# Three value loads put behind a later gate, and one copy put behind two loads, in a fused window-attention and feed-forward kernel

## The chip, the cores and the metric

The kernel runs on one core of a Trainium2 chip. The metric is the device time in microseconds (us) of one execution. Before the change three runs took 278.83, 281.04 and 281.4 us; the median is 281.04 us. The numbers of an engine's work come from one profiled execution.

The core has a matrix engine (TensorE, PE in the profile; its weight loads are PEld), a vector engine (VectorE, DVE), a scalar engine (ScalarE, ACT), a general engine (GpSimd, POOL) and a sync engine (SyncE, SP) that issues transfers. POOL and SP each work through their instructions in program order, and each issues DMAs (transfers) to a queue of its own. Both queues are served by the same 16 DMA engines.

## The reference

`q`, `k`, `v` have 8 batches, 8 heads, 576 positions and 64 values per head. Attention is limited to a window of 32 positions either side; its result, as 4608 rows of 512, goes through a two-layer feed-forward block:

```python
scores = q @ k.T / 8          # per batch and head
scores = where(abs(i - j) <= 32, scores, -1e9)
attn   = softmax(scores)
x      = (attn @ v).transpose(0, 2, 1, 3).reshape(4608, 512)
h      = x @ w_in                                  # 512 -> 2048
g      = h * sigmoid(1.702 * h)
out    = g @ w_out                                 # 2048 -> 512, float32
```

## The kernel before, in words

The 4608 rows are cut into 36 *units* of 128 rows and 9 *tiles* of 512 rows, four units each, numbered from 0. The kernel is one long program in which tile `t`'s first layer, tile `t-1`'s second layer and the attention of tile `t+1` are woven together by hand, so that PE always has something to multiply. The order on every engine is the order in which the program text emits it; waits are semaphores.

**Loads (POOL's queue).** For each unit, `load_kq` (line 144) brings 128 rows of queries or keys into a staging tile `qst` or `kst`, cast to 16 bits, and `load_v` (line 214) brings values into one of nine tiles `ve`. A unit that crosses a batch border takes two transfers. Each block of 64 queries needs keys and values of 128 positions, and the second block of a unit is offset by 64 rows; so values are needed a second time in shifted form: `odd_v(u)` (line 233) lets POOL copy half of unit `u`'s values and half of unit `u+1`'s into a tile `vo`, in two copies. It can run only when both units' values have landed.

**Transposes (SP's queue).** `turn(u)` has SP issue two DMA transposes (line 250): staged queries of `u` to `qT`, staged keys of `u+1` to `kT`. The normalized attention output `xn` is also transposed by SP's DMAs (line 447) into `xT`, four per tile, one per unit. SP's stores of finished output (line 613) stand in the same queue.

**A tile's round.** For `t` from 2 on, `front(t)` (not for `t = 2`) computes the scores of tile `t+1`'s four units, amid second-layer products, and emits `x_sums(t)` (lines 495 and 496): four DVE subtractions of quarters of `xT`, called `xs`, which the first layer of tile `t` multiplies. Then `back(t)` goes through four first-layer groups `n = 0..3` (`l1_group`). A group starts with a product from `xT`, then some second-layer work, then a product from `xs`. In group `n = 2` it first emits `values_four` (attention times values of tile `t+1`; `pv` in the profile, with `ve` and `vo` as operands), and `norm_four`, which normalizes into `xn` and emits the four `xT` transposes.

**The gates.** After a group, POOL makes a one-element copy `seen` (line 943) from a tile that DVE writes during the group (`gs`, line 510). POOL can't pass it before that group is that far. Behind the gate stand the loads of the table `LOADS`, by `(t, n)` or, where there is no such key, by `n`; the numbers in it count from `u = 4t + 4`. For `t = 2` (`u = 12`), ahead of the groups `n = 0` and `n = 1`, `ahead("kq", ...)` emits loads of queries 17 and keys 18, and of queries 18 and 19 with keys 19 and 20; just before `back(2)`, the three odd copies of units 13, 14 and 15.

The third tile is `t = 2`; its fourth group is `n = 3`. Units 12 to 15 are the attention of tile 3, units 16 to 19 that of tile 4. The first use of odd copy 15 is in `values_four(12)`; of values 16 to 20 and odd copies 16 to 19, in `values_four(16)`.

Of the kernel before, what the change touches and what calls it, by code (L numbers as in the profile page):

```python
# [26 lines left out]
class _Kernel:  # L27
# [689 lines left out]
    def opening(self):  # L717
# [95 lines left out]
        for u in (8, 9, 10, 11):  # L813
# [29 lines left out]
        self.x_T2(6, "t", act)  # L843
        self.do(self.l2, 5)

    LOADS = {(2, 1): [("kq", 8)], (2, 2): [("v", 5, 6, 7)], (2, 3): [("v", 8), ("kq", 9), ("odd", 4), ("kq", 10)],
# [25 lines left out]
    @staticmethod  # L872
    def do(fs, n=99):
        for _ in range(min(n, len(fs))):
            fs.pop(0)()
# [28 lines left out]
    def back(self, t):  # L904

        more = t + 1 < self.NT
        do, l2 = self.do, self.l2
        u = 4 * t + 4
        bands = [lambda i=i: self.band(u + i) for i in range(4)] if more else []
        dv = bands  # L910
        for n in range(4):
            for i in {2: ((4,), (5,), (6, 7), ()), 3: ((4, 5), (6, 7), (), (8,))}.get(t, ((5, 6), (7,), (), (8,)))[n]:
                self.turn(u + i)
            if t == 2:
                self.ahead("kq", *((17,), (18, 19), (), ())[n])
            if more and n == 2:
                self.values_four(u)
                self.norm_four(u, ("A", "C", "E"), (0, 1))
                do(l2, 1)

            key = n if more else ("last", n)
            if t == 2:
                key = ("first", n) if n < 2 else n
            share = dict(zip((1, 7, 2, 4), self.SHARES.get(key, (3, 3, 5, 5))))

            def fill(i):
                do(l2, share[i])
                self.l2eng = self.nc.scalar
                if i == 4 or more and (n, i) == (1, 7):
                    do(dv, 99 if i == 4 else 2)  # L930

            def side(i):
                if more and n == 2:
                    self.norm_four(u, (f"t{i}",), (2 + i,))
                else:
                    do(dv, 1)

            self.l1_group(t, n, fill, side)
            dv += self.g_sums(t, 2 * n, 2)
            if more and (t > 2 or n > 0):  # L940
                if u + n + 7 <= self.NU:
                    c = 2 * ((n - 1) % 4) + 1
                    self.nc.gpsimd.tensor_copy(self.seen, self.gs[t - (n == 0)][0:1, 2, c, 255:256])  # L943
                for what, *us in self.LOADS.get((t, n)) or self.LOADS[n]:
                    for i in us:
                        if what == "odd":
                            self.spread(u + i)
                        else:
                            self.ahead(what, u + i)
        return dv  # L950

    def run(self):
        pool, act = self.nc.gpsimd, self.nc.scalar
        self.l2eng, self.seed2 = self.nc.vector, act
        more = self.l2 = self.layer2_plain(0, 0) + self.layer2([(i, j) for i in range(self.NT) for j in range(2)][1:-1],
                                                               (self.NT - 1, 1))
        self.opening()
        self.do(self.x_sums(1))
        late = self.first_layer1()
        do = self.do  # L960
        dve = self.nc.vector
        do(more, 8)
        self.scores_two(8, ("t", "AC"))
        exps = self.scores(10, "BE", True)
        self.turn(14)
        self.turn(15)
        do(late)
        do(more, 4)
        self.band_two(8)
        self.l2eng = act  # L970
        do(more, 16)
        do(exps)
        do(more, 8)
        self.values(8, "t")
        self.values(9, "AC")
        self.odd_v(12, pool)
        self.scores(11, "BE")
        self.norm(8)
        pool.tensor_copy(self.seen, self.pair[8][0:1, 0, 1, 0, 0:1])
        for u in (14, 15, 16):  # L980
            self.load_v(u)
        self.ahead("kq", 16)
        self.band(10)
        self.norm(9)
        do(more, 12)
        self.scores_two(12, ("t", "BE"))
        self.values(10, "AC")
        self.band(11)
        self.norm(10)
        do(more, 6)  # L990
        self.values(11, "t")
        self.norm(11)
        do(more, 4)
        self.scores(14, "BE")
        self.x_T2(8, "A", dve)
        self.x_T2(10, "C", dve)
        self.scores(15, "t")
        do(more, 6)
        do(self.x_sums(2))
        self.seed2 = self.l2eng = dve  # L1000
        for u in (13, 14, 15):
            self.odd_v(u, pool)
        late = self.back(2)
        for t in range(3, self.NT):
            self.front(t, late)
            late = self.back(t)
        self.l2eng = act
        self.do(late, 2)
        self.do(self.l2, 16)
        self.do(late)  # L1010
        self.do(self.l2, 999)
# [77 lines left out]
```

## Time and profile before

| | |
|---|---|
| median of three runs | 281.04 us (278.83 to 281.4) |
| profiled execution, device time | 280.49 us |
| its span, first to last instruction | 278.7 us |
| PE busy | 265.3 us (95%) |
| DVE busy | 213.9 us (77%) |
| ACT busy | 195.3 us (70%) |
| POOL busy | 140.1 us (50%) |
| POOL's DMA queue | 18.42 MB in 107,200 packets |
| SP's DMA queue | 18.23 MB in 43,664 packets |
| granted TensorE clock | 1.00 |

Times in the profile are microseconds from the start of the span, unless marked ns. A row of a timeline gives start, length, engine, line, operation, what is written and read, a count (xN) of instructions merged, and in brackets the idle time of the engine before it with what ended it. A row of the chain of work that ended last gives start, length and what it was. The engine name with a small q (SPq) is that engine's issue of a DMA, not its transfer; the transfer's time from issue to landing is in the DMA answers.

### The profile page before, as it was taken

How to read it: one execution, taken by the hardware profiler on the slowest of the kernel's cores; microseconds unless marked ns; L12 is line 12 of the kernel's file. 1: busy time of each engine (PE TensorE's matmuls, PEld its weight loads, DVE VectorE, ACT ScalarE, POOL GpSimd, SP SyncE). 2: the span in 40 equal slices, each digit the busy share in tenths (PEclk: the TensorE clock that was granted, in tenths of full speed). 3: DMA queues.
4: the chain of work that ended last, by engine and by line, in shares of the span. 5: the costliest groups of instructions: out<-in, count | busy, mean ns of one | idle time of the engine just before them, and what ended most of it. 6: DMA issues, size and time to landing. Idle time of an engine off the chain costs nothing.

```text
span 278.7 us, 8814 instructions
## 1 busy us (share of the span) xinstructions
PE 265.3 (95%) x3604; PEld 221.6 (80%) x3604; DVE 213.9 (77%) x497; ACT 195.3 (70%) x345; POOL 140.1 (50%) x219
## 2 busy tenths in 40 slices
PE   1989999999999998999999999999999999999994
PEld 1567556898888886888888888888888888888883
DVE  3664998988898878878887887888788878855631
ACT  2585885999886697568956896698569856577420
POOL 8994597995984289629741974295430000000000
PEclk9999999999999999999999999999999999999999
DMA  7999999999999999999999999999992023202033
GB/s 86 165 201 195 181 206 163 159 155 162 195 99 162 169 138 197 177 199 114 164 138 195 126 153 132 209 140 146 173 96 78 2 80 73 78 0 78 0 116 115
DMA packets 151353, 37.74 MB, mean 135 GB/s; under 512 B 138640, under 2 KB 146960, under 8 KB 151312
## 3 DMA queue, kind: packets, MB, share of 16 engines
q0 software_dynamic: 107200, 18.42, 96.6%
q1 hardware_dynamic: 43664, 18.23, 34.1%
q8 instruction: 28, 0.46, 0.7%
q10 hardware_dynamic: 448, 0.52, 0.6%
q14 instruction: 13, 0.11, 0.1%
HBM read 36.83 MB, written 9.44 MB: 166 GB/s over the span
## 4 chain that ended last, share of the span: by engine, by line
PE 87%; DMA 6%; DVE 2%; ACT 2%; POOL 1%; issue 1%; POOLq 0%; DVEq 0%
PE o L71 39%; PE h L71 37%; PE sc L71 5%; PE pv L71 4%; DMA o_sb<-in_k_dram 4%; DMA xT<-xn 3%; PE tp L180 1%; PE tp L259 1%; ACT kq L68 1%; PE tp L463 1%; POOL kq L155 1%; ACT L803 0%; POOL vo L233 0%; PE tp L204 0%; DVE xn L398 0%
## 5 line engine op out<-in xcount | busy, mean ns | idle before, releaser
L579 ACT ACTIVATE g<-h 128x512 f16<-128x512 f32 x128 | 72.1, 598 | 38.0 <-PE h L71 31.7
L71 PEld LDWEIGHTS <-g 128*128 128x128 f16 x568 | 54.6, 98 | 7.8
L71 PE MATMUL h<-xs,a 128*128 128x256 f16 x384 | 57.6, 272 | 1.1 <-DVE xs L495 1.1
L71 PEld LDWEIGHTS <-a 128*128 128x128 f16 x512 | 49.5, 98 | 10.2 <-DVE xs L495 1.9
L71 PE MATMUL h<-xT,w 128*128 128x256 f16 (+1 forms) x352 | 53.7, 283 | 0.2 <-DMA w<-in_moe_w_in_dram 0.2
L71 PEld LDWEIGHTS <-w 128*128 128x128 f16 x480 | 45.8, 98 | 9.1 <-DMA w<-in_moe_w_in_dram 0.5
L71 PE MATMUL o<-w,g 128*128 128x256 f16 (+1 forms) x304 | 49.9, 284 | 0.0
L233 POOL COPY vo<-ve 64x264 int32<-64x264 int32 x71 | 35.5, 500 | 19.8 <-DMA ve<-in_v_dram 16.5
L71 PEld LDWEIGHTS <-gs 128*128 128x128 f16 x416 | 39.9, 98 | 5.3
L71 PE MATMUL o<-b,gs 128*128 128x256 f16 x280 | 43.3, 273 | 0.0
L71 PE MATMUL o<-b,g 128*128 128x256 f16 x264 | 38.6, 273 | 0.0
L592 DVE TENSOR_TENSOR h<-h,s 128x512 f32<-128x512 f32 x32 | 22.4, 699 | 18.4 <-PE h L71 17.7
L214 POOL DMA_DIRECT2D ve<-in_v_dram x39 | 33.2, 862 | 2.8 <-issue 1.5
L144 POOL DMA_DIRECT2D qst<-in_q_dram x35 | 28.2, 810 | 1.3 <-issue 1.3
L598 DVE TENSOR_TENSOR h<-h,s 128x512 f32<-128x512 f32 x32 | 22.3, 698 | 7.6 <-PE h L71 7.5
L144 POOL DMA_DIRECT2D kst<-in_k_dram x31 | 26.6, 862 | 1.4 <-DMA w<-in_moe_w_out_dram 1.4
L68 ACT COPY h<-h 128x512 f32<-128x512 f32 x32 | 18.8, 588 | 10.9 <-PE h L71 9.9
L293 ACT ACTIVATE p<-sc 128x512 bf16<-128x512 f32 x48 | 24.7, 624 | 0.6 <-PE sc L71 0.6
L943 POOL COPY seen<-gs 1x1 f16<-1x1 f16 x17 | 3.3, 196 | 35.8 <-DVE gs L510 35.8
L68 ACT COPY o_sb<-o 128x256 f32<-128x256 f32 (+1 forms) x25 | 11.7, 467 | 12.6 <-PE o L71 12.6
L68 ACT COPY s<-h 128x512 f32<-128x512 f32 x32 | 19.1, 596 | 1.8 <-PE h L71 1.2
L71 PE MATMUL h<-xs,w 128*128 128x256 f16 x128 | 19.2, 273 | 0.0
(102 smaller groups left out, 387.8 us busy)
## 6 DMA issues: line engine op xcount, KB each, us to landing
out_dram<-o_sb SPq DMA_DIRECT2D x33, 256.0 KB, 4.1
ve<-in_v_dram POOLq DMA_DIRECT2D x31, 128.0 KB, 6.6
kst<-in_k_dram POOLq DMA_DIRECT2D x25, 128.0 KB, 6.0
qst<-in_q_dram POOLq DMA_DIRECT2D x21, 128.0 KB, 5.2
w<-in_moe_w_out_dram POOLq DMA_DIRECT2D x4, 512.0 KB, 10.4
w<-in_moe_w_in_dram POOLq DMA_DIRECT2D x4, 256.0 KB, 8.8
w<-in_moe_w_in_dram POOLq DMA_DIRECT2D x2, 512.0 KB, 10.9
qst<-in_q_dram POOLq DMA_DIRECT2D x7, 96.0 KB, 6.8
```

Source lines behind the costliest of these rows:

```text
L68: (eng.copy if eng is self.nc.scalar else eng.tensor_copy)(out, in_)
L71: self.nc.tensor.matmul(out, lhsT, rhs, start=start, stop=stop, skip_group_check=True)
L144: self.nc.gpsimd.dma_start(t[off:off + n], src[b, :, s:s + n, :].rearrange("h s d -> s h d"))
L155: self.nc.gpsimd.dma_start(self.stage["first"][0:n // j, :, at:at + j], src[0, :, lo:lo + n, :].rearrange("h (p j) d -> p h j d", j=j))
L180: self.nc.tensor.transpose(tp[64 * (h % 2):64 * (h % 2) + 64, h // 2, x, :], src[:, 4 * i + h, at + x, :], self.ident[r, r])
L214: self.nc.gpsimd.dma_start(t[off:off + n, :, :self.D], self.v[b, :, s:s + n, :].rearrange("h s d -> s h d"))
L233: eng.tensor_copy(*((words(vo[64:128]), words(self.ve[u % 9][64:128])), (words(vo[0:64]), words(nxt)))[i])
L293: exps = [lambda eo=eo: self.nc.scalar.activation(p[:, eo].rearrange("k h s -> k (h s)"), sc[eo], AF.Exp, scale=self.scale) for eo in rang ...
L579: act.activation(g[:, f, 256 * half:256 * half + 256], bank.rearrange("p (i n) -> p i n", i=2), AF.Gelu_apprx_sigmoid)
L592: dve.tensor_add(e, b, s7)
L598: dve.tensor_add(c, b, s7)
L943: self.nc.gpsimd.tensor_copy(self.seen, self.gs[t - (n == 0)][0:1, 2, c, 255:256])
```

## The change

Values of units 17, 18 and 19 (numbers 5, 6, 7 in the table) are no longer loaded behind the gate that follows group `n = 2` of tile 2, but behind the next gate, which follows `n = 3`, ahead of the loads that were there. The gate after `n = 2` keeps its one-element copy and has nothing behind it; the lookup is rewritten so that an empty list is taken as such. The odd copy of unit 15 leaves the row of three copies ahead of `back(2)` and is emitted after the loads of queries 17 and keys 18.

```diff
-    LOADS = {(2, 1): [("kq", 8)], (2, 2): [("v", 5, 6, 7)], (2, 3): [("v", 8), ("kq", 9), ("odd", 4), ("kq", 10)],
+    LOADS = {(2, 1): [("kq", 8)], (2, 2): [], (2, 3): [("v", 5, 6, 7, 8), ("kq", 9), ("odd", 4), ("kq", 10)],
              (3, 0): [("kq", 7), ("odd", 1, 2, 3), ("v", 5)],
@@ back
             if t == 2:
                 self.ahead("kq", *((17,), (18, 19), (), ())[n])
+                if n == 0:
+                    self.odd_v(15, self.nc.gpsimd)
@@ back, behind the gate
-                for what, *us in self.LOADS.get((t, n)) or self.LOADS[n]:
+                for what, *us in self.LOADS.get((t, n), self.LOADS[n]):
@@ run, ahead of back(2)
-        for u in (13, 14, 15):
+        for u in (13, 14):
             self.odd_v(u, pool)
```

## The prediction

> **What bounds the kernel now.** The page's chain of work that ended last comes first: it names the engine that has to get shorter.
>
> ```profile
> PE 87%; DMA 6%; DVE 2%; ACT 2%; POOL 1%; issue 1%; POOLq 0%; DVEq 0%
> ```
>
> PE is the path; another edit counts only where PE stands still. The waits of PE between 40 and 274 us have one row, and PE's timeline shows its place:
>
> ```profile
> PE h L71 <- DVE xs L495: 1.1, 1, 1.1
> ...
> 103.72 0.60 PE L71 MATMUL h<-xT,w 128*128 128x256 f16 x4
> 104.15 0.60 PE L71 MATMUL o<-w,g 128*128 128x256 f16 x4
> 105.90 0.61 PE L71 MATMUL h<-xs,a 128*128 128x256 f16 x4 [1.15 <-DVE xs L495]
> ```
>
> So in some 230 us PE has one hole, at the start of tile 3's first group: the first product from `xs` waits for DVE's subtraction. DVE's timeline and the chain tell what DVE waited for:
>
> ```profile
> 105.42 0.42 DVE L495 TENSOR_TENSOR xs<-xT 128x512 f16<-128x512 f16 x1 [2.00 <-DMA xT<-xn]
> ...
> 98.30 7.03 DMA xT<-xn
> ```
>
> The fourth transpose of tile 3's `xT` was issued at 98.30 and landed 7.03 later. The full price of the hole comes from the period between one tile's `pv` and the next, all with the same work, in the chain:
>
> ```profile
> 87.37 1.17 PE pv L71 x63
> 116.26 1.17 PE pv L71 x63
> 143.74 1.17 PE pv L71 x57
> 171.16 1.17 PE pv L71 x64
> ```
>
> 28.89 us, then 27.48 and 27.42. The first period, which holds the hole, is **1.41** us longer. (The bracket says 1.15 because PE's ends are modelled with an overlap.) I take 1.41; 1.15 is the lower bound.
>
> **Why that transpose was slow.** SP's and POOL's timelines and the answers by line on 447, for this tile and the next (first and last issue; then landing, min/median/max):
>
> ```profile
> 91.91 1.67 SPq L250 DMA_TRANSPOSE kT<-kst  x1
> 93.67 5.85 SPq L447 DMA_TRANSPOSE xT<-xn  x4
> 96.26 2.63 POOL L214 DMA_DIRECT2D ve<-in_v_dram  x3 [0.29 <-issue]
> 99.81 0.24 POOL L943 COPY seen<-gs 1x1 f16<-1x1 f16 x1 [0.93 <-DVE gs L510]
> ...
> 124.74 0.18 POOL L943 COPY seen<-gs 1x1 f16<-1x1 f16 x1 [5.29 <-DVE gs L510]
> L447 SPq DMA_TRANSPOSE xT<-xn x4: 1216/1345/1707, 93.7 to 98.3; - x4
> DMA to landing us min/median/max: 3.9/5.7/7.0
> L447 SPq DMA_TRANSPOSE xT<-xn x4: 1195/1234/1877, 118.9 to 123.8; - x4
> DMA to landing us min/median/max: 3.8/4.2/5.8
> ```
>
> Values 17 to 19 are issued at 96.26 to 98.89, in the middle of the four transposes (93.67 to 99.52). One tile later POOL is idle for 5.29 us up to 124.74, while these transposes are issued, and they land in 3.8 to 5.8 us.
>
> **The change, part by part.**
>
> *Values 17 to 19 leave the gate at 95.80.* Behind the later gate (99.81) the first of them is issued at about 100.33, 2.0 us after the last transpose instead of 2.0 before. With 3.8 to 5.8 us that transpose lands at 102.1 to 104.1. DVE reaches the subtraction at 103.41 (the row before ends there, 105.42 - 2.00), and PE wants its result at 104.15 + 0.44 = 104.6. With a landing at 104.1 some 0.1 is left of the hole, below that none. **Gain 1.41**, bounds 1.15 and 1.47 (28.89 - 27.42). What is late next there: ACT, still in the copy that the group's third product adds to, which ends at 105.38:
>
> ```profile
> 104.69 0.69 ACT L68 COPY h<-h 128x512 f32<-128x512 f32 x1
> ```
>
> Ahead of that third product stand four matmuls from `xs` and five of the second layer, nine at 0.11 (0.44 for four, from 103.72 to 104.15), so it comes at 105.6. The copy is covered by 0.2 us.
>
> *What they push.* POOL's timeline behind the gate at 99.81:
>
> ```profile
> 100.33 0.88 POOL L214 DMA_DIRECT2D ve<-in_v_dram  x1 [0.27 <-issue]
> 103.50 0.85 POOL L233 COPY vo<-ve 64x264 int32<-64x264 int32 x2
> 106.63 0.90 POOL L144 DMA_DIRECT2D qst<-in_q_dram  x1
> 107.51 0.89 POOL L144 DMA_DIRECT2D kst<-in_k_dram  x1
> 108.45 4.59 POOL L233 COPY vo<-ve 64x264 int32<-64x264 int32 x6
> 112.99 0.88 POOL L214 DMA_DIRECT2D ve<-in_v_dram  x1
> 115.81 0.18 POOL L943 COPY seen<-gs 1x1 f16<-1x1 f16 x1 [1.95 <-DVE gs L510]
> ```
>
> POOL has no idle time from 100.33 to 113.87, so all of it moves back by the three issues, 2.63 us: the odd copy of unit 16, queries 22 and 23 with keys 23 and 24, and the odd copies of 17 to 19 (now from 111.08). The gates that follow waited 1.95 (115.81) and 5.29 (124.74); the second swallows the delay even with PE 1.41 earlier, so later tiles don't see it. Two consumers stand before that.
>
> (a) *Odd copies 17 to 19 and `pv` of tile 4.* `pv` starts at 116.26 - 1.41 = 114.85, and unit 19, the last quarter of 1.17 us, is wanted at 115.73. The six copies take 4.59 (as now) or six times 0.43 = 2.55 (half of the 0.85 above): they end at 113.6 to 115.7. In front, odd 16 now waits for values 17, which were issued at 100.33. The nearest landings are 4.4 (the same load in its old place) and 7.6 (values 19):
>
> ```profile
> ve<-in_v_dram POOLq DMA_DIRECT2D x1, 128.0 KB, 4.4
> ve<-in_v_dram POOLq DMA_DIRECT2D x1, 128.0 KB, 7.6
> ```
>
> That is 104.7 to 107.9, and POOL gets there at 106.13: a wait of 0 to 1.8, behind which stand queries 22 and everything after. I take the lower end, since values 17 are again the first of a burst. Cost **0**, with up to 115.7 + 1.8 - 115.73 = 1.8 as the bound.
>
> (b) *SP's transposes of queries 21 to 23 and keys 22 to 24.* They wait for the landing of loads now 2.63 later, and `xT` of tile 4 stands behind them in SP's queue:
>
> ```profile
> 116.21 1.21 SPq L250 DMA_TRANSPOSE kT<-kst  x1
> 118.86 6.20 SPq L447 DMA_TRANSPOSE xT<-xn  x4
> qst<-in_q_dram POOLq DMA_DIRECT2D x1, 128.0 KB, 8.1
> kst<-in_k_dram POOLq DMA_DIRECT2D x1, 128.0 KB, 7.9
> 132.28 0.42 DVE L495 TENSOR_TENSOR xs<-xT 128x512 f16<-128x512 f16 x1
> 132.82 0.44 PE h L71 x4
> 133.70 0.44 PE h L71 x4
> ```
>
> Queries 23 and keys 24, issued at 106.63 and 107.51, took 8.1 and 7.9 in a queue filled by values 17 to 19 ahead of them. Issued at 109.26 and 110.14 and landing in 6.2 to 8.1, they let SP start the last two transposes 0.6 to 2.5 us later than now, and `xT` at 119.5 to 121.4. The fourth of them comes 4.9 later (118.9 to 123.8 now), at 124.4 to 126.3, and lands in 3.8 to 7.0: 128.2 to 133.3. PE wants `xs` at 133.70 - 1.41 = 132.29, DVE's part takes 0.58 (105.32 to 105.90), so it must have landed by 131.7. Cost **0** in the middle (130.7), up to 1.6 at the bound.
>
> *The odd copy of unit 15 behind two loads.*
>
> ```profile
> 76.84 0.86 POOL L233 COPY vo<-ve 64x264 int32<-64x264 int32 x2 [0.61 <-DMA ve<-in_v_dram]
> 78.51 0.67 POOL L233 COPY vo<-ve 64x264 int32<-64x264 int32 x1 [0.81 <-DMA ve<-in_v_dram]
> 79.13 1.37 POOL L144 DMA_DIRECT2D qst<-in_q_dram  x2
> ```
>
> Its second half waits 0.81 for values 16 while three DMAs stand behind it. Now they go at 77.3 instead of 79.13, the two copies fall at about 79.5 to 80.4 with nothing to wait for, and the loads after them go some 0.9 earlier. Its consumer is `pv` at 87.37: 7 us of cover. SP goes from its last transpose (91.91, for 1.67) straight to `xT` at 93.67, so `xT` may start up to 0.9 earlier; that is in the same direction as the first part, and worth nothing once the hole is closed. Cost and gain 0.
>
> Sum: 280.49 - 1.41 = **279.1** by the profiled execution. Its 280.49 lies below the median 281.04; the middle of the four known times is 280.8, so I add 0.3: **279.4**.
>
> **The rivals.**
>
> *R1, the hole moves one tile on.* If (b) comes out near its far end, `xT` of tile 4 lands late and PE waits at 132.3. For it: the margin there, now 133.1 less 127.6 to 129.6, falls to about 1, and tile 4's transposes would again stand beside a burst of loads (behind the gate at 124.74, less 1.41). Against: it takes slow transposes on top of slow loads. Price 0 to 1.6, of which I take 1.0: 280.4.
>
> *R2, the change doesn't reach its aim.* The fourth `xT` could be late for its neighbours on SP's own queue; then it lands at 105.3 as before and the time stays at 280.8. Against: in the next tile the same four, just as close, landed in at most 5.8. The Trainium skill's "DMA: Bandwidth & Descriptors", section "Anatomy of one DMA", puts a POOL load at about 2.0 us plus bytes over 436 GB/s; for 128 KB that is 2.3 us, so that values 17 to 19 would be gone by 101.2 and could not hold a transpose until 105.3. This trace's 4.4 to 7.6 us speak against that figure.
>
> *R3, slower.* The wait of odd 16 for values 17 comes out at its end, 1.8: the copies 17 to 19 end at 117.5, PE stands 1.8 in `pv`, and SP's chain is 1.8 later as well, for another 1.6 at tile 4's `xs`. Net -1.41 + 3.4 = +2.0: 282.8 with the 0.3. It decides from values 17 landing after 106.1, or six copies that take over 4.65 us. For it: hardly a margin in (a) at 4.59. Against: values 17 are first of a burst, as where they took 4.4, and a pair of copies elsewhere takes 0.85. The Trainium skill's "SBUF — State Buffer", section "Who interferes with whom", says that a VectorE operation with two SBUF inputs and a GpSimd operation that reads SBUF shut each other out for a whole instruction; the trace agrees as far as six copies took 4.59 and two 0.85, but what the six will meet after the move no row shows.
>
> **How the numbers follow.** Forecast 60%, R1 18%, R2 10%, R3 12%. A difference of 1% (2.8 us) is about what a measurement of this kernel can tell from no change; the forecast gain is half of that. The range holds the forecast, R1 and R2 with the scatter of the runs (278.83 to 281.4, that is 2.0 below and 0.6 above the middle): 279.4 - 1.4 = 278.0 to 280.8 + 0.6 = 281.4. R3 is left out. Faster by over 1% (below 278.2) needs the scatter's low end on top of the gain: 8%. Slower by over 1% (above 283.9) needs R3 at its bound and more: 8%. Within: 84%.
>
> **What would show it.** PE's waits between 40 and 274 us empty, with a `pv` period of 27.4 in place of 28.89; the fourth `xT` of tile 3 landing in under 6 us; the odd copies 17 to 19 ending between 113.6 and 115.7; `xT` of tile 4 first issued at 119.5 to 121.4. The prediction is wrong if PE waits for POOL at `pv` near 115 or for DVE near 132, or if the hole at 105 stays with no value load in flight.

## The result and the profile after

The changed kernel took a median of **281.8 us** (280.31 to 285.88, 22 runs) against 280.31 us before (278.63 to 284.07, 22 runs). The ratio is **1.0058**, with a 95% interval of 1.0038 to 1.0079: slower by 1.6 us, where 1.4 us faster was forecast; the median lies 0.4 above the range of 278.0 to 281.4. This ratio, like those in the table further down, leaves out the runs in a slower state, here two of the 22 (285.27 and 285.88 us). The profiled execution has a span of 281.5 us (278.7 before).

The waits of PE between 40 and 274 us, the whole view; before, it had one row:

```profile
PE h L71 <- DVE xs L495: 2.0, 1, 2.0
PE o L71 <- issue: 1.0, 1, 1.0
PE pv L71 <- POOL vo L233: 0.9, 2, 0.5
PE sc L71 <- issue: 0.2, 1, 0.2
```

PE's timeline gives their places (one row of the `pv` work of tile 4 that did not wait comes first):

```profile
115.58 0.22 PE L71 MATMUL pv<-ve,p 128*64 128x65 bf16 x1
...
116.73 0.19 PE L71 MATMUL pv<-vo,p 128*64 128x65 bf16 x1 [0.40 <-POOL vo L233]
...
117.64 0.19 PE L71 MATMUL pv<-vo,p 128*64 128x65 bf16 x1 [0.46 <-POOL vo L233]
...
136.25 0.61 PE L71 MATMUL h<-xs,a 128*128 128x256 f16 x4 [2.02 <-DVE xs L495]
```

The hole at 105 is gone. In its place PE waits twice for the odd copies in tile 4's `pv`, and 2.02 us for `xs` of tile 4, one tile after the place that the change mended. The chain of work that ended last shows what these waits hang on:

```profile
88.22 1.17 PE pv L71 x62
...
103.72 9.85 DMA ve<-in_v_dram
113.87 0.87 POOL kst L144
114.79 0.54 POOL vo L233
...
128.52 7.15 DMA xT<-xn
135.76 0.44 DVE xs L495
136.25 0.61 PE h L71 x4
...
146.61 1.17 PE pv L71 x64
...
174.03 1.17 PE pv L71 x61
```

From tile 3's `pv` to tile 4's are 115.58 - 88.22 = 27.36 us (28.89 before), and from tile 4's to tile 5's 146.61 - 115.58 = 31.03 (27.48 before). So 1.53 is gained and 3.55 lost: **+2.0** over the two periods. The next one is 27.42, as before. The remaining 0.85 of the spans' difference lies ahead of 88.22 (87.37 before); PE's 1.0 of "issue", idle time for which the profile shows no wait, stands at 79.6, so in that stretch; the kernels that follow have such a row or not, without a pattern that was found.

The chain's fourth value load, values 20, took 9.85 us. In the waits of POOL between 40 and 274 us a row has come that was not there:

```profile
POOL kst L144 <- DMA ve<-in_v_dram: 2.9, 1, 2.9
```

A load of keys waits for a load of values, with which it shares no data. POOL's timeline and, below it, SP's, in the stretch in question:

```profile
101.13 3.50 POOL L214 DMA_DIRECT2D ve<-in_v_dram  x4 [0.22 <-issue]
...
106.92 0.85 POOL L233 COPY vo<-ve 64x264 int32<-64x264 int32 x2
...
110.06 0.90 POOL L144 DMA_DIRECT2D qst<-in_q_dram  x1
113.87 0.87 POOL L144 DMA_DIRECT2D kst<-in_k_dram  x1 [2.92 <-DMA ve<-in_v_dram]
114.79 2.79 POOL L233 COPY vo<-ve 64x264 int32<-64x264 int32 x6
```

```profile
102.60 0.81 SPq L613 DMA_DIRECT2D out_dram<-o_sb  x2
103.51 2.20 SPq L250 DMA_TRANSPOSE qT<-qst  x1
105.81 1.26 SPq L250 DMA_TRANSPOSE kT<-kst  x1
114.27 1.20 SPq L250 DMA_TRANSPOSE qT<-qst  x1
...
121.80 1.21 SPq L250 DMA_TRANSPOSE kT<-kst  x1
...
124.20 5.51 SPq L447 DMA_TRANSPOSE xT<-xn  x4
```

POOL stands still from 110.96 to 113.87, and the six copies of odd 17 to 19 begin at 114.79 and end at 117.58, two us after `pv` has begun. SP stands still from 107.07 to 114.27, until queries 21 have landed, and then runs its transposes almost without a break into `xT` at 124.20. The answers on the DMAs issued in two narrow windows, around 104 and around 105, give the landings of values 20 and of queries 21:

```profile
ve<-in_v_dram POOLq DMA_DIRECT2D x1, 128.0 KB, 9.9
qst<-in_q_dram POOLq DMA_DIRECT2D x1, 128.0 KB, 9.6
```

Before, the same two loads were issued 3.4 us earlier, landed after 5.6 and 6.3, and SP issued the transpose of queries 21 at 107.55 (the answer for the window 101.1 to 103, then SP's timeline):

```profile
ve<-in_v_dram POOLq DMA_DIRECT2D x1, 128.0 KB, 5.6
qst<-in_q_dram POOLq DMA_DIRECT2D x1, 128.0 KB, 6.3
```

```profile
107.55 1.19 SPq L250 DMA_TRANSPOSE qT<-qst  x1
```

### The profile page after: what moved, and what is told of

It is laid out like the page before. It is cut to its first block, busy times and chain, and to the rows that moved or that the text cites. A ratio compares the mean times of both kernels' runs of the same rounds, so it can differ in the third digit from the quotient of the medians.

```text
span 281.5 us, 8814 instructions
## 1 busy us (share of the span) xinstructions
PE 265.5 (94%) x3604; PEld 221.9 (79%) x3604; DVE 213.7 (76%) x497; ACT 195.2 (69%) x345; POOL 139.6 (50%) x219
## 4 chain that ended last, share of the span: by engine, by line
PE 82%; DMA 6%; DVE 3%; POOL 3%; issue 2%; ACT 2%; POOLq 0%; DVEq 0%
PE h L71 36%; PE o L71 35%; PE sc L71 4%; PE pv L71 4%; DMA ve<-in_v_dram 4%; DMA xT<-xn 3%; POOL vo L233 1%; PE tp L180 1%; PE tp L259 1%; ACT kq L68 1%; PE tp L463 1%; POOL kq L155 1%; DVE xn L398 1%; POOL ve L214 1%; ACT L803 0%
## 5 line engine op out<-in xcount | busy, mean ns | idle before, releaser
L71 PE MATMUL h<-xs,a 128*128 128x256 f16 x384 | 57.6, 272 | 2.0 <-DVE xs L495 2.0
L233 POOL COPY vo<-ve 64x264 int32<-64x264 int32 x71 | 34.6, 487 | 23.6 <-DMA ve<-in_v_dram 20.3
```

The source lines that it names most:

```text
L71: self.nc.tensor.matmul(out, lhsT, rhs, start=start, stop=stop, skip_group_check=True)
L233: eng.tensor_copy(*((words(vo[64:128]), words(self.ve[u % 9][64:128])), (words(vo[0:64]), words(nxt)))[i])
```

## The experiments

For each kernel the table gives the ratio to the kernel before on the same chip (with its 95% interval), the stretch from tile 3's `pv` to tile 5's in the profiled execution, read from the chain, and the waits of PE in that stretch. Two periods without a wait take 54.9 (27.48 + 27.42). The last row is a kernel that leaves out some of the output; "values earlier" has no entries since its profile is no measure of them, for the reason given there. Each profile is a single execution.

| kernel | ratio | two periods, us | PE waits at: `xs` of tile 3; `pv` of tile 4; `xs` of tile 4 |
|---|---|---|---|
| before | 1 | 56.4 | 1.15; 0; 0 |
| changed | 1.0058 (1.0038 to 1.0079) | 58.4 | 0; 0.86; 2.02 |
| odd copy only | 0.9978 (0.9949 to 1.0007) | 57.0 | 1.54; 0; 0 |
| values only | 1.0053 (1.0021 to 1.0084) | 58.4 | 0; 0.46; 2.29 |
| a small load more | 1.0008 (0.9968 to 1.0049) | 56.9 | 0; 0.38; 1.18 |
| queries and keys first | 1.0237 (1.0200 to 1.0275) | 64.2 | 0; 5.67; 0 |
| values earlier | 1.0052 (1.0017 to 1.0088) | | |
| queries 21 first | 1.0048 (1.0008 to 1.0088) | 58.7 | 0; 0.48; 2.70 |
| two loads | 0.9971 (0.9936 to 1.0005) | 56.2 | 0; 0; 1.00 |
| one load | 0.9936 (0.9897 to 0.9975) | 55.3 | 0; 0; 0 |
| one load, again | 0.9991 (0.9950 to 1.0032) | 55.6 | 0.42; 0; 0 |
| one load and odd copy | 0.9969 (0.9932 to 1.0005) | 54.9 | 0; 0; 0 |
| transposes later | 1.0058 (1.0013 to 1.0102) | 57.6 | 0; 0; 2.34 |
| without a store | 0.9931 (0.9894 to 0.9969) | 54.9 | 0; 0; 0 |

The theory after the result, called Q in the expectations: the value loads push POOL's queue, and two consumers of it are late. Where an edit below empties an entry of the table `LOADS`, the changed lookup goes with it.

### The two halves of the change

Only the odd copy moved:

```diff
+                if n == 0:
+                    self.odd_v(15, self.nc.gpsimd)
...
-        for u in (13, 14, 15):
+        for u in (13, 14):
```

> The kernel before, with the odd copy of unit 15 moved and the value loads left where they were. Theory Q (the value loads push POOL's queue, and two consumers of it are late; the odd copy has no part): the hole of 1.4 us before tile 3's first xs product stays, PE waits nowhere else, pv periods 28.9, 27.4, 27.4; time within 0.2% of before. Rival O (the moved copy and the earlier loads and transposes behind it cost the time): 1.2 to 1.6 us slower than before, with a later first xT of tile 3 or a PE wait ahead of 90 us.

No difference is told: 0.9978, the interval includes 1. The hole stays, at 1.54. Rival O falls by the time, and PE waits nowhere else. The first `xT` of tile 3 does come later, at 95.34 for 93.67, which rival O had named as a sign; but it comes at 94.89 too in the next kernel, where the odd copy stays in its place.

Only the value loads moved:

```diff
-    LOADS = {(2, 1): [("kq", 8)], (2, 2): [("v", 5, 6, 7)], (2, 3): [("v", 8), ("kq", 9), ("odd", 4), ("kq", 10)],
+    LOADS = {(2, 1): [("kq", 8)], (2, 2): [], (2, 3): [("v", 5, 6, 7, 8), ("kq", 9), ("odd", 4), ("kq", 10)],
```

> The kernel before, with values 17 to 19 behind the later gate and the odd copy of unit 15 left where it was. Theory Q: all of the loss is here; 1.2 to 2.0 us slower than before, hole before tile 3's xs closed, PE waits of 0.5 to 1.0 us for POOL at tile 4's pv and of about 2 us for xs of tile 4, and POOL waits about 3 us for the landing of values 20 before it may issue keys 24. Rival O: no slower than before, about 1.4 us faster.

The whole loss is here: 1.0053 and 58.4 us, the same as with both. From the waits in this kernel between 40 and 274 us:

```profile
POOL kst L144 <- DMA ve<-in_v_dram: 2.5, 1, 2.5
...
PE h L71 <- DVE xs L495: 2.3, 1, 2.3
...
PE pv L71 <- POOL vo L233: 0.5, 1, 0.5
```

All three new waits come again, though the one at `pv` is half as long (0.46 for 0.86), and PE's "issue" row at 79 us does not come: the loss of the two periods doesn't need it.

### What POOL waits for ahead of keys 24

```diff
+        self.small = cst.tile([16, 64], F16, name="small")
...
-    LOADS = {(2, 1): [("kq", 8)], (2, 2): [], (2, 3): [("v", 5, 6, 7, 8), ("kq", 9), ("odd", 4), ("kq", 10)],
+    LOADS = {(2, 1): [("kq", 8)], (2, 2): [], (2, 3): [("v", 5, 6, 7, 8), ("kq", 9), ("odd", 4), ("small", 0), ("kq", 10)],
...
-                        if what == "odd":
+                        if what == "small":
+                            self.nc.gpsimd.dma_start(self.small, self.w_in[0:16, 0:64])
+                        elif what == "odd":
```

> The changed kernel with one more, tiny load (16 rows of 64 values into a tile that nothing reads) issued by POOL ahead of queries 22. It asks what POOL waits for ahead of keys 24. Theory S (a transfer of POOL's queue waits for the landing of the one eight issues before it): the wait for values 20 moves from keys 24 to queries 23, 2 to 4 us, and keys 24 then wait for queries 21, under 1 us. Rival K (keys 24 wait for their staging tile): the wait stays at keys 24 and queries 23 don't wait.

POOL's timeline in this kernel:

```profile
107.63 0.52 POOL L950 DMA_DIRECT2D small<-in_moe_w_in_dram  x1
108.14 1.38 POOL L145 DMA_DIRECT2D qst<-in_q_dram  x2
110.04 0.89 POOL L145 DMA_DIRECT2D kst<-in_k_dram  x1 [0.52 <-DVE p L368]
110.93 0.43 POOL L946 COPY seen<-gs 1x1 f16<-1x1 f16 x1
112.26 0.88 POOL L145 DMA_DIRECT2D qst<-in_q_dram  x1 [0.91 <-DMA ve<-in_v_dram]
113.14 0.88 POOL L145 DMA_DIRECT2D kst<-in_k_dram  x1
```

The wait for `ve` has moved from keys 24 to queries 23, one issue earlier, as theory S has it; keys 24 wait for nothing. Its size was missed, 0.91 for 2 to 4, since values 20 landed after 8.0 us here; with it the waits of PE are smaller too, and the two periods 56.9. So in this program a load of POOL isn't issued before the load eight issues ahead has landed. The semaphores that the traces record with each instruction say why: POOL's loads tell of their landing by eight semaphores in turn, numbers 99 to 106; a load is held until the last landing told by its own semaphore has come; and in the changed kernel values 20 and keys 24 both have 106. In the kernel before the same tie was there and held nobody up: values 20 were down at 105.9 and keys 24 were issued at 107.51.

### Which consumer costs what

Queries 21 to 23 and keys 22 to 24 ahead of the values:

```diff
-    LOADS = {(2, 1): [("kq", 8)], (2, 2): [], (2, 3): [("v", 5, 6, 7, 8), ("kq", 9), ("odd", 4), ("kq", 10)],
-             (3, 0): [("kq", 7), ("odd", 1, 2, 3), ("v", 5)],
+    LOADS = {(2, 1): [("kq", 8)], (2, 2): [], (2, 3): [("kq", 9), ("kq", 10)],
+             (3, 0): [("kq", 7), ("v", 1, 2, 3, 4), ("odd", 0, 1, 2, 3), ("v", 5)],
```

> The changed kernel, with queries 21 to 23 and keys 22 to 24 issued ahead of values 17 to 20 behind the later gates, and odd copies 16 to 19 after these. It parts the two consumers. Theory Q: SP's transposes are on time, xT of tile 4 is first issued at 119 or earlier in the time of before, and PE no longer waits for xs of tile 4 (under 0.3 us); the odd copies end at about 116, so that PE waits 0.3 to 1.5 us for POOL at tile 4's pv; 0 to 1 us faster than before. Rival L (the late odd copies also make xT late, and the order of the loads does nothing for it): both waits as in the changed kernel or larger, 1.5 us or more slower than before.

It does part the two: the wait at `xs` of tile 4 is gone, and all of the loss is in `pv`. But the time was missed by far, 2.4% slower for 0 to 1 us faster. PE's timeline:

```profile
116.81 0.19 PE L71 MATMUL pv<-vo,p 128*64 128x65 bf16 x1 [2.55 <-POOL vo L233]
...
118.30 0.21 PE L71 MATMUL pv<-vo,p 128*64 128x65 bf16 x1 [1.02 <-POOL vo L233]
...
119.97 0.21 PE L71 MATMUL pv<-vo,p 128*64 128x65 bf16 x1 [1.03 <-POOL vo L233]
...
121.70 0.21 PE L71 MATMUL pv<-vo,p 128*64 128x65 bf16 x1 [1.07 <-POOL vo L233]
```

Unit after unit, PE waits for an odd copy, and the copies for a value load: issued at 105.95 to 108.9, these took 10.4 to 12.3 us to land, behind the loads of queries 21 to 23 and keys 22 to 24 and beside SP's transposes. The expectation had the odd copies end at about 116; the last ended at 121.64.

Only queries 21 and keys 22 ahead of the values:

```diff
-    LOADS = {(2, 1): [("kq", 8)], (2, 2): [], (2, 3): [("v", 5, 6, 7, 8), ("kq", 9), ("odd", 4), ("kq", 10)],
-             (3, 0): [("kq", 7), ("odd", 1, 2, 3), ("v", 5)],
+    LOADS = {(2, 1): [("kq", 8)], (2, 2): [], (2, 3): [("kq", 9), ("v", 5, 6, 7, 8), ("kq", 10)],
+             (3, 0): [("kq", 7), ("odd", 0, 1, 2, 3), ("v", 5)],
```

> The changed kernel, with queries 21 and keys 22 ahead of values 17 to 20 and odd copy 16 put beside 17 to 19. In the changed kernel SP stood still until queries 21 landed and then ran its transposes without a break up to tile 4's xT. Theory Q: queries 21 land at about 106 and their transpose is issued at 108 or earlier, but queries 22 land late in their place (about 115); tile 4's first xT at 120 to 122 and the wait at its xs 0 to 1.2 us; the wait at pv under 1.0 us; 0 to 1.0 us faster than before, 1.5 to 2.5 us faster than the changed kernel. Rival P (the odd copies are what makes xT late): wait at xs as in the changed kernel, about 2 us.

Theory Q's numbers fail here: 1.0048 and a wait of 2.70 at `xs`, more than in the changed kernel. Queries 21 landed in 3.6 us and were transposed at 107.4, but the value loads behind them then took 8.7 to 9.7 and queries 22 9.5 to 9.8, so that `xT` was first issued at 125.1. To put one pair of loads first moves the lateness to the next pair; `xT` needs all of the queries and keys to come through, and only with all six ahead of the values, in the kernel above, was the wait at `xs` gone. Rival P's number came out, but not its reason: the transposes waited for loads, not for the odd copies.

### How many loads

Both start from the kernel before: values 18 and 19 behind the later gate, or values 19 alone.

```diff
-    LOADS = {(2, 1): [("kq", 8)], (2, 2): [("v", 5, 6, 7)], (2, 3): [("v", 8), ("kq", 9), ("odd", 4), ("kq", 10)],
+    LOADS = {(2, 1): [("kq", 8)], (2, 2): [("v", 5)], (2, 3): [("v", 6, 7, 8), ("kq", 9), ("odd", 4), ("kq", 10)],
```

```diff
-    LOADS = {(2, 1): [("kq", 8)], (2, 2): [("v", 5, 6, 7)], (2, 3): [("v", 8), ("kq", 9), ("odd", 4), ("kq", 10)],
+    LOADS = {(2, 1): [("kq", 8)], (2, 2): [("v", 5, 6)], (2, 3): [("v", 7, 8), ("kq", 9), ("odd", 4), ("kq", 10)],
```

> The kernel before, with values 18 and 19 behind the later gate, values 17 left where they were. Theory Q: between one and three loads: the hole at tile 3's xs under 0.5 us, a wait of 0.3 to 1.5 us at tile 4's xs and up to 0.5 us at its pv; within 0.8 us of before on either side. Rival C: as before, with the hole still at 1 us or more.

> The kernel before, with values 19 alone behind the later gate: POOL's queue behind it moves by one issue (0.9 us) instead of three. Theory Q: tile 4's first xT comes 0 to 2 us later than before and lands in time, so no wait at tile 4's xs or under 0.5 us, and none at its pv; the hole at tile 3's xs shrinks but stays, 0.3 to 1.0 us; 0 to 1.0 us faster than before. Rival C (each load beside SP's traffic costs the same wherever it stands): hole and new waits sum to as much as before, no difference.

> Values 19 alone behind the later gate, once more: 0.5 to 1.8 us faster than before, and no PE wait of over 0.3 us at the xs or pv of tiles 3 and 4. Rival C: no difference from before.

SP's row of tile 4's `xT` with one load, then with two, then PE's row with two:

```profile
119.53 5.57 SPq L447 DMA_TRANSPOSE xT<-xn  x4
```

```profile
121.95 5.50 SPq L447 DMA_TRANSPOSE xT<-xn  x4
```

```profile
134.04 0.61 PE L71 MATMUL h<-xs,a 128*128 128x256 f16 x4 [1.00 <-DVE xs L495]
```

With one load no PE wait is left in the first of two profiles, and 0.42 at `xs` of tile 3 in the second. With two the hole is closed, and 1.00 comes back one tile on; with three it is 2.0 to 2.3, with `pv` besides. Behind tile 4's `pv` the first `xT` starts after 2.6 us in the kernel before (118.86 - 116.26), then with one, two and three loads after 4.8, 6.3 and 8.6; 1.1 of the first step is `pv` itself coming earlier (27.77 after tile 3's, for 28.89). Rival C falls by the traces with one load, where the waits are 0 and 0.42 for the 1.15 of before. With two the hole is closed, against rival C, but the new wait of 1.00 makes up for it. The expectations for one load missed too: the hole was to stay at 0.3 to 1.0 in the first kernel and was gone, and the repeat was to be faster by 0.5 us or more and without a wait over 0.3. By the clock, one load is 0.9936 in the first measurement and not told from 1 in the second (0.9991); both parts with one load:

> The kernel before, with values 19 alone behind the later gate and the odd copy of unit 15 behind the loads of queries 17 and keys 18: both parts of the change, the first with one load in place of three. Theory Q: as with values 19 alone, no PE wait at the xs or pv of tiles 3 and 4, 0.2 to 1.5 us faster than before; the odd copy adds nothing that can be told.

0.9969, interval up to 1.0005, with 54.9 us in the two periods and no wait over 0.1 us in them. That makes three measurements with one load, this one with the odd copy moved too: all below 1, one of them clear. Some 0.3% faster than the kernel before is my estimate from the three, which these runs don't settle. All three intervals lie below that of the change as made.

### Loading earlier instead of later

```diff
-    LOADS = {(2, 1): [("kq", 8)], (2, 2): [("v", 5, 6, 7)], (2, 3): [("v", 8), ("kq", 9), ("odd", 4), ("kq", 10)],
+    LOADS = {(2, 1): [("kq", 8)], (2, 2): [], (2, 3): [("v", 8), ("kq", 9), ("odd", 4), ("kq", 10)],
...
                 self.ahead("kq", *((17,), (18, 19), (), ())[n])
+                if n == 1:
+                    self.ahead("v", 17, 18, 19)
```

> The kernel before, with values 17 to 19 loaded not later but earlier: ahead of tile 2's second group, right behind keys 20, in some 2 us in which POOL has no work. Theory Q: nothing behind the later gate moves, the transposes of tile 3's xT run without value loads beside them, the hole closes to under 0.3 us and no new wait comes; 1.1 to 1.4 us faster than before. Rival T (the transposes are slow for what stands beside them on SP's own queue, or the loads now slow the transposes ahead of xT just as much): the hole stays at 0.8 us or more, time as before.

1.0052 (1.0017 to 1.0088): slower. Theory Q fails here, and rival T, which had the time of before, doesn't meet it either. The profiled execution took 288.31 us, 4.8 over the kernel's median, so that its trace is no measure of the waits; why it is slower was not settled.

### What made the loads land late

SP's transposes of queries 20 and keys 21 put behind the others:

```diff
-            for i in {2: ((4,), (5,), (6, 7), ()), 3: ((4, 5), (6, 7), (), (8,))}.get(t, ((5, 6), (7,), (), (8,)))[n]:
+            for i in {2: ((4,), (5,), (6, 7), ()), 3: ((5,), (6, 7, 4), (), (8,))}.get(t, ((5, 6), (7,), (), (8,)))[n]:
```

> The changed kernel, with SP's transposes of queries 20 and keys 21 put behind those of queries 23 and keys 24, so that none runs beside the loads of values 17 to 20. It asks what made values 20 land after 9.9 us. Theory X (SP's transposes beside them): values 20 land in 7 us or less, POOL's wait ahead of keys 24 is under 0.5 us, and PE's wait for POOL at tile 4's pv is gone or under 0.3 us; the wait at tile 4's xs stays, since as many transposes stand ahead of xT. Rival Y (the store of finished output that is issued at the same time): values 20 still land after 8.5 us or more and POOL still waits 2 to 3 us.

And the changed kernel without the store that SP issues at 102.6:

```diff
     def store(self, t, pr, o):
+        if (t, pr) == (1, 1):
+            return
```

> The changed kernel without the one store (256 rows of output, the second half of tile 1) that SP issues at 102.6, beside the value loads; these rows of the output are left out. Theory X: values 20 still land after 8 us or more, POOL still waits 1.5 us or more ahead of keys 24. Rival Y: values 20 land in 7 us or less and POOL hardly waits.

The DMA answers for values 20, first with the transposes put later, then without the store:

```profile
ve<-in_v_dram POOLq DMA_DIRECT2D x1, 128.0 KB, 5.9
```

```profile
ve<-in_v_dram POOLq DMA_DIRECT2D x1, 128.0 KB, 4.6
```

Each brings the landing from 9.9 to under 7, and with it POOL's wait ahead of keys 24 and PE's wait in `pv` go. So X and Y each hold in what they foretold for their own kernel, and neither alone is the cause: the loads land as late as 9.9 when store, transposes and loads come in the same 5 us, and not with one of the two moved or left out. The two can't be weighed against each other by these runs. The kernel without the store also loses the time that SP stands still ahead of it: the two transposes behind it were then issued at 97.7 and 99.0, before the value loads, where they were issued at 103.5 and 105.8.

With the transposes later the wait at `xs` of tile 4 stays, at 2.34, as expected, and the total doesn't move (1.0058): what PE saves in `pv` is within the interval, and `xT` is no earlier. Without the store both waits are gone, and that kernel, which writes 512 KB less, shows the two periods, 54.9, that the forecast was after.

## Why the prediction was wrong

**Right: what the change was to mend.** The hole was a transpose slowed by value loads: with these moved, the fourth `xT` of tile 3 landed in 4.3 us in place of 7.0, and the period is 27.36, a gain of 1.53 for the 1.41 of the sum. By the answer on line 447, landings min/median/max, in the changed kernel:

```profile
DMA to landing us min/median/max: 2.5/3.9/4.9
```

Rival R2 is refuted by that, and by the kernel with the odd copy alone, where the value loads stayed and these landings were 6.3 to 7.3. For the odd copy of unit 15 no cost or gain was told, as costed. But the loads behind it did not go earlier as the working had it, 77.3 for 79.13: they went at 80.13 (79.54 with the odd copy alone), since the copies ahead of them still waited for values, in the changed kernel 0.70 and 1.67.

**The step that failed: "What they push", with (a) and (b) in its wake.** "All of it moves back by the three issues, 2.63 us" took POOL as a list of issues, with the landings of the kernel before behind it, and put the cost at 0. It held up to queries 23, issued 110.06 - 101.13 = 8.9 us after the first load, for 109.26 - 100.33 = 8.9 by the working. Then came a wait that stands nowhere in the working: keys 24 could not be issued before values 20 had landed. And the landings grew. The longest among the working's bounds for these loads was 8.1; values 20 and queries 21 took 9.9 and 9.6. The sum held the loads' durations fixed while putting three more of them beside SP's store and two transposes. What it put at 0 was 3.55 us.

For (a), the six copies took 2.79 us, near the lower end of 2.55 to 4.59, but they began at 114.79, not 111.08; the wait of 2.92 and the later start of 0.85 make up that difference within 0.1. The wait of odd 16 for values 17, which R3 turned on, did not come: these landed 3.7 us after issue, at 104.8, and POOL got there at 106.92. The six copies now ran beside DVE's work from 115.31 on, whose large operands are `o` and `pv` in PSUM, with one operation of two SBUF inputs (`gs` from `g` and `gs`, at 114.65) at their start; before, they had run beside four operations on `p` and `mask`, both in SBUF, between 108.35 and 112.2. The Trainium skill's "SBUF — State Buffer", section "Who interferes with whom", by which a VectorE operation with two SBUF inputs and a GpSimd operation that reads SBUF shut each other out, fits that.

For (b), the working tied `xT` to the last of the loads, queries 23 and keys 24. It was the first that decided: queries 21 landed at 114.2, and the six transposes and a store that SP then issues take until 124.20. That is 2.8 after the end of the range, 121.4, that the working gave; 0.85 of it is the later start. The margin at `xs` was used up, and PE waited 2.02 for a bound of 1.6.

**The rivals.** R1 and R3 both came, together. That R3's sum, +2.0, is the two periods' +2.0 is luck: the wait it named, of odd 16 for values 17, did not come, and the waits of PE that it put at 1.8 and 1.6 were 0.86 and 2.02. R1's bound of 1.6 was passed as well. They were given 18% and 12% as alternatives to the forecast, though both hang on the same landings and would rise or fall together. The range has a slip at its lower end, which had no part in the miss: it takes 1.4 off the forecast, where the scatter that it names is 2.0 below the middle.

By the Trainium skill's "DMA: Bandwidth & Descriptors", section "Anatomy of one DMA", a load of 128 KB was estimated at 2.3 us. None of these loads came down to it; the shortest is 3.5, at the head of the burst in the kernel with the values alone moved.

## What to carry to other kernels

A load that is moved out of one burst joins another: cost it with that burst's landings lengthened, not with the landings it had, and go through what shares the DMA engines there (stores and transposes of other queues too). Look in the trace for the tie between a transfer and one issued some places before it; slack of 1.6 us hid it here until a landing grew by 4.3. And move as little as closes the hole: with one load of three it was gone in two profiles and 0.42 in a third, and the other two loads bought the loss. The page of the kernel before held a warning, in its row of the busy share of the 16 DMA engines:

```profile
DMA  7999999999999999999999999999992023202033
```

Each digit is the tenths of one of 40 slices of the span. From 7 to 209 us every slice is at 90% or more, so that room for a burst was not to be taken for granted. What this share counts beside the moving of data the page doesn't tell.

## What was not expected of the hardware

In the stretch studied here, the profile of the values moved earlier left aside, a 128 KB load of many short rows took from 3.5 to 12.3 us to land, with the same bytes and the same queue, by what stood ahead of it and beside it. One and the same load went from 9.9 to 4.6 with one store of 512 KB left out (and two transposes earlier with it), and to 5.9 with two transposes moved later.

PE stood still for 0.2 to 1.0 us somewhere between 72 and 80 us in seven of the thirteen profiles of the changed kernel and its variants, for "issue", with no wait that the profile shows. The profile of the kernel before has none of it, and neither has that of the values moved alone. It was not tried what that is.
